# A Strassen FNet and MLP mix on one Trainium2 core: right-hand sums by adding DMAs, stored sums of x, and three more couples split twice

## The chip, the cores and the metric

The kernel runs on one core of a Trainium2 chip. Its time is the device time of one execution in microseconds (us), the median of several. The engines of the core that appear here are TensorE (PE, matmuls into PSUM), VectorE (DVE), ScalarE (ACT), GpSimd (POOL) and SyncE (SP). Here POOL and SP only issue DMAs, each from a queue of its own that runs in order; DVE, ACT and PE have in-order queues as well.

## The reference

```python
def reference(x, Cr, Ci, Wr, Wi, w1, b1, w2, b2, gate_w):     # x: 2048 x 1024, F = 3584
    g = sigmoid((x * gate_w).sum(-1, keepdims=True))
    a, b = x @ Wr.T, x @ Wi.T                                  # hidden transform, 1024 x 1024 each
    y = Cr @ a - Ci @ b                                        # sequence transform, 2048 x 2048 each
    h = relu(x @ w1 + b1) ** 2
    return g * y + (1 - g) * (h @ w2 + b2)                     # all float32
```

## The kernel before, in words

**Four products, five stages.** x W gives `ab` (x times both hidden matrices), C multiplies `ab` with the sequence matrices, K being real and imaginary part one behind the other (4096), the two h stages give h from w1 (2048 and 1536 features) and x, O multiplies w2 with h (K 3584). Intermediate results (`ab`, `gy`, `h`) go to HBM tiles and come back.

**Tiles.** A tile is 128 partitions x 2 x 512 float32, 512 KB, in one of 55 SBUF slots. It holds a K-step of 256 (2 x 128) by 512 rows or columns. Each operand tile is split into `hi` (rounded to fp32r, by ACT) and `lo` (what is left, by DVE; `Operand`, line 278 on), and each product is three matmuls: hi hi, hi lo, lo hi. Results gather in four pairs of PSUM banks (`Group`, line 337); ACT or DVE take them out.

**Strassen's form by Winograd.** Every stage cuts its matrices 2 x 2 and computes seven products instead of eight (`FACTORS`, line 40). The left factors need the sums S1 to S4 of left blocks, the right ones T1 to T4 of right blocks (`SUMS_L`, `SUMS_R`, lines 36 to 39); `Sums.of` (line 402) makes each once, as a `Part` (line 225): load two tiles (or one, if the other is a sum in SBUF), add or subtract on DVE. `T2` of C and O is written to an HBM tile `copy` by POOL and loaded again later (`FAR_TALL`). `seven` (line 425) runs the products in the order 1, 2, 5, 6, 3, 7, 4, and says how each is added to the four blocks of the result: a running value is put into PSUM ahead of the matmuls by ACT (`onto`), or added when the banks are taken out.

**Twice.** Some products are cut a second time by the same rule (`twice`). In `wide` (x W and h) these are products 1, 2, 5, 3 and 4, whole. In `tall` (C and O, where K is long) `TWICE_C` and `TWICE_O` say for how many couples of K-steps each product is cut again; the K-steps left over are done directly. Before, C has 1, 4, 4, 4 couples in products 1, 2, 3, 4 (of 8 K-steps), O 2, 3, 3, 3 (of 7). A couple cut again works with operands half as wide: names `both`, which hold hi and lo side by side.

**What sets the order.** The code records all operations first (`Queue`, line 123). `plan` (line 973) gives each a due time from its place ahead of the matmul that needs it, simulates the engines with the constants of lines 27 to 30, hands out the slots in that order, and writes down the order of each engine's queue; `emit` builds it. So any change of an operation or of a constant moves many others, and nothing is reordered at run time. Loads are issued by SP, stores by POOL. A store that nothing reads again (those of `out`) is due 20 us behind its place.

Of the kernel before, what the change touches and what calls it, by code (L numbers as in the profile page):

```python
# [44 lines left out]
def gated_mix_kernel(ctx: ExitStack, tc: tile.TileContext, x4, xn, w4, ct, w1a, w1b, w2, b1, b2, gw, out):  # L45
# [53 lines left out]
    class Op:  # L99


        def __init__(self, engine, name, args, kwargs):
            self.engine, self.name, self.args, self.kwargs = engine, name, args, kwargs
            sights = [a for a in (*args, *kwargs.values()) if isinstance(a, Sight)]
            outs = [a for a in (args[0], kwargs.get("accum_out")) if isinstance(a, Sight)]
            self.ins, self.outs = [a for a in sights if not any(a is o for o in outs)], outs
            n = max([a.size() for a in sights] + [0])
            self.load, self.end = 0.0, 0.0
            if name == "dma_start":
                self.time, self.load = ISSUE[engine], n * P * 4 / RATE[0]  # L110
            elif engine == "tensor":
# [113 lines left out]
    class Part(Near):  # L225


        def __init__(self, a, b=None, op=None, width=512):
            super().__init__("part")
            self.blocks, self.op, self.width, self.copy = ([a] if b is None else [a, b]), op, width, None  # L230
# [15 lines left out]
        def load(self, engines):  # L246
            run(self.load_parts(engines))

        def make_parts(self):
            for b in self.blocks:  # L250
                assert not isinstance(b, (Near, View)) or b.done
            src = [b.slot if isinstance(b, (Near, View)) else t for b, t in zip(self.blocks, self.slots)]
            mine = [t for t in self.slots if t is not None]
            self.slot, self.done = mine[0] if mine else take("sum"), True
            for k, c in self.cuts:
                if self.op:
# [138 lines left out]
    class Sums:  # L395


        def __init__(self, get, sums, keep=False, far=()):

            self.get, self.sums, self.keep, self.far, self.made = get, sums, keep, far, {}  # L400

        def of(self, key, width=512, near=False):
            if key in self.made:
                return self.made[key]
            if key not in self.sums:
# [4 lines left out]
            else:  # L410
                a, b, op = self.sums[key]
                e = Part(*(self.of(p, width).far() if p in self.far and not near else self.of(p, width) for p in (a, b)), op, width)
# [12 lines left out]
    def seven(order, second, new_u, c11, c12, c21, c22, put, add, direct, twice, slots, sign=1):  # L425

        one, u = new_u(), new_u()
        before = {p: order[:order.index(p)] for p in order}

        def product(p, old, new, ends, slots, drop=False, sign=1):  # L430
            if p in second:
                twice(p, old, new, ends, drop, sign)
                return

            direct(p, old, slots, lambda k, ps: put(new, k, ps, ends, sign), [new], sign, drop)
# [5 lines left out]
        def seven(k, ps):  # L441
            add(c22, k, ps, True, None, sign)
            if 4 in before[7]:
                add(c21, k, ps, True)
            else:
                put(u, k, ps)

        ends = {}
        for p in order:
# [6 lines left out]
            elif p == 4 and 7 in before[4]:  # L456
                product(4, u, c21, True, slots, True)
            elif p == 4:
                product(4, None, c21, False, slots)
            elif p == 5:  # L460
                product(5, None, c22, False, slots, sign=sign)
            elif p == 6:
                direct(6, one, 2 * slots, six, [u, c12], 1, 2 in before[6])
            else:
                direct(7, u, slots * (4 not in before[7]), seven, [u, c22, c21], 1, True)
# [5 lines left out]
    def tall(left, right, ksteps, order, second, first, target, final, last=None):  # L471
# [8 lines left out]
        right = {(q, c): Sums(lambda j, n, q=q, c=c: right_(j, n, q, c), SUMS_R, far=FAR_TALL) for right_ in (right,)  # L480
# [4 lines left out]
        def put(dst, k, ps, ends=False, sign=1):  # L485
            near = dst[k]
            near.slot or near.new()
            if ends:
# [4 lines left out]
            near.begun = True  # L493

        def add(dst, k, ps, ends=False, src=None, sign=1):
            near = dst[k]
            near.slot or near.new()
            nc.vector.tensor_tensor(flat(near.slot), flat((src or dst)[k].slot), flat(ps), op=ADD)
            near.begun = True
            if ends:  # L500
# [3 lines left out]
        def direct(p, onto, slots, take_up, into, sign, spend=False):  # L504
# [6 lines left out]
                            onto=onto and [onto[c, rp] for rp in range(2)], spend=spend, by_row=end and c) for c in range(2)]  # L511
            sts = {q: left[q].operand(l) for q in range(ksteps)}
            for q, c in sorted(((q, c) for q in range(ksteps) for c in range(2)), key=lambda e: e[::-1] if end else e):
                step(sts[q], right[q, c].operand(r), groups[c])
                if p == 6 and q < 2 * second.get(4, 0):
                    steps[-1][3].append(right[q, c].early("T4"))

        def twice(p, old, new, ends, drop, sign):
# [5 lines left out]
            if rest and (not old or p in first):  # L524
                some = [Group(4, len(rest), (lambda rp, ps, c=c: put(new, (c, rp), ps, sign=sign), 2 * (old is not new),
                                             [new[c, rp] for rp in range(2)]),
                              onto=old and [old[c, rp] for rp in range(2)], spend=drop) for c in range(2)]
# [4 lines left out]
                old, rest, drop = new, (), False  # L532
# [10 lines left out]
            l2 = {q: Sums(lambda m, j, q=q: View(base[j, q], 256 * m), SUMS_L, True) for q in range(k)}  # L543
            r2 = {q: Sums(lambda j, c, q=q: right[2 * q + j, c].of(r), SUMS_R, True) for q in range(k)}

            def one(_, ps):
                if old:
                    tmp[0, 0].new()
                    nc.scalar.activation(flat(tmp[0, 0].slot), flat(ps), AF.Copy)
                    add(new, block(0, 0), ps, src=old)  # L550
# [5 lines left out]
            def onward(dst, key, ps):  # L556

                if old:
# [3 lines left out]
                    nc.vector.tensor_tensor(flat(at), flat(old[key].slot), flat(u), op=ADD)  # L562
# [16 lines left out]
            def five(_, ps):  # L579
                key = block(1, 1)  # L580
                add(new, block(0, 1), ps)
                if old:
                    at = new[key].slot or new[key].new()
                    nc.vector.tensor_tensor(flat(at), flat(old[key].slot), flat(ps), op=ADD)
# [5 lines left out]
                    if ends and not more:  # L590
# [25 lines left out]
            for q in range(k):  # L616
                again = Sums(lambda j, c, q=q: right[2 * q + j, c].of(r), SUMS_R, True)
# [22 lines left out]
    def wide(left, right, rows, order, second, target, final, sign=1, onto_old=False):  # L640
# [9 lines left out]
        left = {(m, q): Sums(lambda i, j, m=m, q=q: left_(i, j, m, q), SUMS_L, far=FAR_WIDE) for left_ in (left,)  # L650
                for m in range(2) for q in range(2)}
        right = {(q, c): Sums(lambda j, n, q=q, c=c: right_(j, n, q, c), SUMS_R, far=FAR_WIDE) for right_ in (right,)
                 for q in range(2) for c in range(2)}
# [6 lines left out]
        def put(dst, k, ps, ends=False, sign=1):  # L660
# [3 lines left out]
            if ends:  # L664
# [4 lines left out]
            near.begun = True  # L669

        def add(dst, k, ps, ends=False, src=None, sign=1):
# [3 lines left out]
            nc.vector.tensor_tensor(view(near.slot, k), view((src or dst)[k].slot, k), view(ps, k),  # L675
                                    op=ADD if sign > 0 else SUB)
            near.begun = True
            if ends:
# [3 lines left out]
        def direct(p, onto, slots, take_up, into, sign, spend=False):  # L682
            l, r = FACTORS[p]
            mvs = [[right[q, c].operand(r) for q in range(2)] for c in range(2)]
            for m in range(2):
                sts = [left[m, q].operand(l, rows * P) for q in range(2)]
                for c in (m, 1 - m):
                    group = Group(rows, 2, (lambda rp, ps, m=m, c=c: take_up((m, c, rp), ps), slots,
                                             [d[m, c, rp] for d in into for rp in range(2)]),
                                  onto=onto and [onto[m, c, rp] for rp in range(2)], spend=spend, sign=sign)  # L690
# [3 lines left out]
        def twice(p, old, new, ends, drop, sign):  # L694

            l, r = FACTORS[p]
            l2 = Sums(lambda m, q: left[m, q].of(l, rows * P), SUMS_L, True)
            r2 = Sums(lambda q, c: right[q, c].of(r), SUMS_R, True)

            def takes(first, m, c, ends=False):  # L700
                def f(rp, ps):
# [3 lines left out]
                    elif old:  # L705
                        add(new, k, ps, ends, old, sign)
# [15 lines left out]
            begin = ((5, other), (1, chain))  # L722
            for p2, group in (*(begin if steps else begin[::-1]), (3, other), (6, chain), (2, last), (7, chain),
# [5 lines left out]
              sign)  # L729

    ab = {(n, q, c): Kept(f"ab{n}{q}{c}") for n in range(2) for q in range(8) for c in range(2)}

    def x_stage():
# [12 lines left out]
        wide(lambda i, j, m, q: x4[2 * i + m, j, q], lambda j, n, q, c: w4[n, c, j, q], 4, WIDE, TWICE_X, target, final, -1, True)  # L748
# [5 lines left out]
    def h_stage(part):  # L754
# [13 lines left out]
        def final(dst, ps, sign):  # L768
            kept, at, tiles, tile0 = to[dst]
            for k in range(tiles):  # L770
# [6 lines left out]
             WIDE, TWICE_H[part], target, final)  # L777
# [56 lines left out]
    def c_stage():  # L834
# [16 lines left out]
        tall(lambda i, j, q: ab[j, q, i], lambda j, n, q, c: ct[n, c, j, q], 8, TALL_C, TWICE_C, FIRST_C, target, final)  # L851
# [3 lines left out]
    def o_stage():  # L855
# [41 lines left out]
        ends = tall(lambda i, j, q: w2[i, j, q], lambda j, n, q, c: h_far[j, q, 2 * n + c], 7, TALL_O, TWICE_O, FIRST_O, target, final, last)  # L897
        return at, rows, fetched, ends
# [12 lines left out]
    at, rows, fetched, ends = o_stage()  # L911
# [61 lines left out]
def plan(ops, count, start):  # L973
# [196 lines left out]
```

## Time and profile before

| | us |
|---|---|
| three runs | 1867.46 median, 1867.27 to 1867.59 |
| the profiled execution | 1867.58 |
| its span, first to last instruction | 1865.3 |
| first wide matmul, from the span's start | 6.45 |
| x W, C, first h, second h, O, each to about | 289, 864, 1142, 1352, 1858 |

The granted clock of TensorE is 0.998 of full speed. The DMA queues moved 445.05 MB, SP's 365.10 and POOL's 78.14. Nearly all instructions carry the line in `emit` where they are built (L1128 before; the changed file is longer, and there it is L1194), so groups are told apart by operation and tile: `sum<-raw` is a sum of two loaded tiles into a third slot, `raw<-raw` one in place, `lo<-raw,hi` the split, `ps<-hi,lo` a matmul, `u`, `h`, `ab`, `y`, `o` results. In the rows, a count stands behind x, a mean time in ns behind the bar's first number, and the idle time of that engine just before, with what ended it, at the end.

### The profile page before, as it was taken

What the parts mean: (1) busy time and instruction counts of PE and PEld (TensorE: products, weight loads), DVE (VectorE), ACT (ScalarE), POOL (GpSimd) and SP (SyncE); (2) the same over time, 40 slices, a digit from 0 to 9 for tenths busy, and PEclk for the clock granted to TensorE, in tenths of its full rate; (3) what the DMA queues carried; (4) which work ended last, traced back from release to release, by engine and by line L of the source; (5) the groups of instructions that cost most, each with busy time, mean ns of one, the idle gap of its engine ahead of it and who ended that gap; (6) DMA issues with size and microseconds to landing.
All of it is one profiled execution on the core that took longest, in us unless ns stands there. A gap on an engine that the chain in (4) does not pass through costs nothing.

```text
span 1865.3 us, 22218 instructions
## 1 busy us (share of the span) xinstructions
PE 1850.1 (99%) x8162; PEld 1528.2 (82%) x8162; DVE 1760.2 (94%) x1728; ACT 1075.9 (58%) x1224; POOL 87.9 (5%) x162
## 2 busy tenths in 40 slices
PE   9999999999999999999999999999999999999998
PEld 7888888888888888888888888788888888888886
DVE  8997999799989899999997999999999999899988
ACT  6474654464343455466585798767976535364442
POOL 0000100000000000000000010000100001000000
PEclk9999999999999999999999999999999999999999
DMA  5741879349897379434552855737664799739943
GB/s 204 255 162 65 341 291 385 136 161 379 297 357 299 122 267 410 183 141 159 203 183 100 313 204 199 254 113 272 252 245 173 289 387 343 281 104 384 371 139 122
DMA packets 128861, 445.05 MB, mean 239 GB/s; under 512 B 14176, under 2 KB 23664, under 8 KB 128752
## 3 DMA queue, kind: packets, MB, share of 16 engines
q1 hardware_dynamic: 106848, 365.10, 53.4%
q0 software_dynamic: 21616, 78.14, 10.6%
q8 instruction: 64, 1.05, 0.2%
q10 hardware_dynamic: 288, 0.39, 0.1%
q14 instruction: 45, 0.37, 0.1%
HBM read 364.92 MB, written 78.65 MB: 238 GB/s over the span
## 4 chain that ended last, share of the span: by engine, by line
PE 84%; ACT 7%; DVE 6%; issue 2%; DMA 1%; SPq 0%; ACTq 0%; DVEq 0%
PE ps L1128 84%; ACT h L1128 3%; ACT hi L1128 3%; DVE lo L1128 2%; DVE h L1128 1%; DVE sum L1128 1%; ACT u L1128 1%; DVE raw L1128 1%; DMA raw<-in_x 1%; ACT ps L1128 0%; DVE o L1128 0%; DMA raw<-in_w 0%; DVE ab L1128 0%; DVE u L1128 0%; SPq L1128 0%
## 5 line engine op out<-in xcount | busy, mean ns | idle before, releaser
L1128 PE MATMUL ps<-hi 128*128 128x512 f32 x2034 | 792.2, 390 | 6.3 <-ACT hi L1128 3.1
L1128 PE MATMUL ps<-hi,lo 128*128 128x512 f32 x2034 | 791.2, 389 | 1.3 <-DVE lo L1128 1.3
L1128 PE MATMUL ps<-lo,hi 128*128 128x512 f32 x2034 | 790.9, 389 | 0.0
L1128 ACT ACTIVATE hi<-raw 128x1024 fp32r<-128x1024 f32 (+2 forms) x384 | 392.7, 1035 | 322.5 <-DVE raw L1128 183.9
L1128 DVE TENSOR_TENSOR lo<-raw,hi 128x1024 fp32r<-128x1024 f32 (+2 forms) x384 | 451.7, 1195 | 15.7 <-ACT hi L1128 10.7
L1128 PEld LDWEIGHTS ps<-hi 128*128 128x128 f32 x2034 | 382.2, 188 | 88.7 <-ACT hi L1128 3.7
L1128 PEld LDWEIGHTS ps<-hi,lo 128*128 128x128 f32 x2034 | 381.9, 188 | 81.7 <-DVE lo L1128 2.2
L1128 PEld LDWEIGHTS ps<-lo,hi 128*128 128x128 f32 x2034 | 382.0, 188 | 79.6 <-DVE lo L1128 0.4
L1128 PE MATMUL ps<-hi,both 128*128 128x512 f32 x1344 | 415.2, 389 | 0.1
L1128 DVE TENSOR_TENSOR raw<-raw 128x1024 f32<-128x1024 f32 (+1 forms) x276 | 324.3, 1203 | 8.6 <-DMA raw<-in_ct 6.3
L1128 ACT ACTIVATE hi<-sum 128x1024 fp32r<-128x1024 f32 x216 | 220.7, 1034 | 180.2 <-DVE sum L1128 121.7
L1128 PEld LDWEIGHTS ps<-hi,both 128*128 128x128 f32 x1344 | 252.2, 188 | 53.2 <-DVE both L1128 0.5
L1128 DVE TENSOR_TENSOR lo<-sum,hi 128x1024 fp32r<-128x1024 f32 (+1 forms) x216 | 254.8, 1195 | 14.5 <-PE ps L1128 12.0
L1128 PE MATMUL ps<-lo,both 128*128 128x512 f32 x672 | 261.4, 389 | 0.0
L1128 DVE TENSOR_TENSOR sum<-raw 128x1024 f32<-128x1024 f32 (+2 forms) x156 | 160.8, 1038 | 17.2 <-PE ps L1128 14.7
L1128 ACT ACTIVATE u<-ps 128x1024 f32<-128x1024 f32 (+1 forms) x116 | 112.4, 972 | 79.9 <-PE ps L1128 62.4
L1128 PEld LDWEIGHTS ps<-lo,both 128*128 128x128 f32 x672 | 126.1, 188 | 26.1
L1128 DVE TENSOR_TENSOR sum<-raw,sum 128x1024 f32<-128x1024 f32 (+2 forms) x117 | 128.4, 1099 | 1.9 <-PE ps L1128 0.6
L1128 DVE TENSOR_TENSOR h<-h,ps 128x1024 f32<-128x1024 f32 (+1 forms) x92 | 98.2, 1081 | 7.4 <-ACT u L1128 5.9
L1128 ACT ACTIVATE both<-sum 128x512 fp32r<-128x512 f32 x96 | 58.7, 623 | 69.9 <-DVE sum L1128 48.9
L1128 ACT ACTIVATE ps<-u 128x1024 f32<-128x1024 f32 (+1 forms) x80 | 78.0, 977 | 23.9 <-DVE u L1128 5.8
L1128 ACT ACTIVATE h<-h,b1c 128x512 f32<-128x512 f32 x112 | 76.1, 710 | 11.2 <-DVE h L1128 11.2
(49 smaller groups left out, 726.5 us busy)
## 6 DMA issues: line engine op xcount, KB each, us to landing
raw<-in_ct SPq DMA_DIRECT2D x153, 512.0 KB, 7.1
raw<-h SPq DMA_DIRECT2D x134, 512.0 KB, 7.1
raw<-in_x SPq DMA_DIRECT2D x107, 512.0 KB, 4.8
raw<-in_w SPq DMA_DIRECT2D x98, 512.0 KB, 6.8
raw<-ab SPq DMA_DIRECT2D x72, 512.0 KB, 7.5
h<-h POOLq DMA_DIRECT2D x48, 512.0 KB, 4.9
raw<-in_w1a SPq DMA_DIRECT2D x36, 512.0 KB, 5.1
ab<-ab POOLq DMA_DIRECT2D x32, 512.0 KB, 6.3
```

What stands on the lines that cost most here:

```text
L1128: made = getattr(real[op.engine], op.name)(*(actual(a) for a in op.args), **{k: actual(v) for k, v in op.kwargs.items()})
```

## The change

- `TWICE_C` and `TWICE_O` get an entry for product 5: two couples in C, one in O. In products cut for some couples only, the remaining K-steps now join the second cut's groups, except in product 2 (`first`).
- The signs of S and T are turned so that T1 and T3 are sums of two blocks as they lie in HBM (the old sums stay as `SUMS_L2`, `SUMS_R2` for the second cut). Products 4 and 6 come out negated, and the code that takes them up subtracts (`less`).
- A sum on the list `lands` is made in one slot: SP loads one tile into it, and when that has landed POOL issues a DMA that adds the second tile from HBM onto it (`accum_op=ADD`). `LAND_X`, `LAND_C`, `LAND_H`, `LAND_O` say for how many of a stage's K-steps and column halves T1 and T3 are made so: 6, 24, 4 and 4, 14, together 52.
- In h the roles of the two sides are exchanged (`flip`), so that x has the S sums in x W and in h. x W stores its sixteen (`shared`, `far`), and the h stages load them.
- The planner prices an adding DMA at 0.85 us of issue and 2.1 times the transfer (`ADDING`), and `out` stores are due 80 instead of 20 us behind their place (`LATE`).

```diff
-TWICE_X, TWICE_C, TWICE_O = (1, 2, 5, 3, 4), {1: 1, 2: 4, 3: 4, 4: 4}, {1: 2, 2: 3, 3: 3, 4: 3}
+TWICE_X, TWICE_C, TWICE_O = (1, 2, 5, 3, 4), {1: 1, 2: 4, 3: 4, 4: 4, 5: 2}, {1: 2, 2: 3, 3: 3, 4: 3, 5: 1}
+LAND_X, LAND_C, LAND_H, LAND_O = {"T1": 4, "T3": 2}, {"T1": 16, "T3": 8}, ({"T1": 4}, {"T1": 2, "T3": 2}), {"T1": 14}
+SHARE = ("S1", "S2", "S3", "S4")
+ADDING = 0.85, 2.1
+LATE = 80.0
-SUMS_L = {"S1": ((1, 0), (1, 1), ADD), "S2": ("S1", (0, 0), SUB), "S3": ((0, 0), (1, 0), SUB),
+SUMS_L = {"S1": ((1, 0), (1, 1), SUB), "S2": ((0, 0), "S1", SUB), "S3": ((1, 0), (0, 0), SUB),
           "S4": ((0, 1), "S2", SUB)}
-SUMS_R = {"T1": ((0, 1), (0, 0), SUB), "T2": ((1, 1), "T1", SUB), "T3": ((1, 1), (0, 1), SUB),
-          "T4": ((1, 0), "T2", SUB)}
+SUMS_R = {"T1": ((0, 1), (0, 0), ADD), "T2": ((1, 1), "T1", ADD), "T3": ((1, 1), (0, 1), ADD),
+          "T4": ((1, 0), "T2", ADD)}
...
         def load(self, engines):
-            run(self.load_parts(engines))
+            if self.lands:
+                self.slots = [take("raw")]
+                a, b = (b.at if isinstance(b, Kept) else b for b in self.blocks)
+                at = self.slots[0][:, :, 0:self.width]
+                next(engines).dma_start(at, a)
+                nc.gpsimd.dma_start(at, b, accum_op=ADD)
+            else:
+                run(self.load_parts(engines))
...
         def of(self, key, width=512, near=False):
             if key in self.made:
                 return self.made[key]
+            if self.shared and key in self.shared:
+                return self.shared[key]
...
+                if self.shared is not None and key in SHARE:
+                    self.shared[key] = e.far()
...
             elif p == 4 and 7 in before[4]:
-                product(4, u, c21, True, slots, True)
+                product(4, u, c21, True, slots, True, less=-1)
...
-                direct(6, one, 2 * slots, six, [u, c12], 1, 2 in before[6])
+                direct(6, one, 2 * slots, six, [u, c12], 1, 2 in before[6], -1)
...
-            if rest and (not old or p in first):
+            if rest and p in first:
...
+        if flip:
+            left = {(m, q): Sums(lambda j, i, m=m, q=q: left_(i, j, m, q), SUMS_R, far=FAR_WIDE, lands=spread(lands, 2 * q + m, 4))
+                    for left_ in (left,) for m in range(2) for q in range(2)}
+            right = {(q, c): Sums(lambda n, j, q=q, c=c: right_(j, n, q, c), SUMS_L, shared=shared[c, q])
+                     for right_ in (right,) for q in range(2) for c in range(2)}
...
-            op.due = op.near + 20.0
+            op.due = op.near + LATE
```

More of the change, by code (lines that the diff above doesn't have):

```diff
@@ L423, in early, with spread, seven, product @@
             return e
-    def seven(order, second, new_u, c11, c12, c21, c22, put, add, direct, twice, slots, sign=1):
+    def spread(lands, i, n):
+        return [key for key, k in lands.items() if (i + 1) * k // n > i * k // n]
+    def seven(order, second, new_u, c11, c12, c21, c22, put, add, direct, twice, slots, sign=1, flip=False):
+        c12, c21 = (c21, c12) if flip else (c12, c21)
         one, u = new_u(), new_u()
         before = {p: order[:order.index(p)] for p in order}
-        def product(p, old, new, ends, slots, drop=False, sign=1):
+        def product(p, old, new, ends, slots, drop=False, sign=1, less=1):
             if p in second:
-                twice(p, old, new, ends, drop, sign)
+                twice(p, old, new, ends, drop, sign, less)
                 return
-            direct(p, old, slots, lambda k, ps: put(new, k, ps, ends, sign), [new], sign, drop)
+            direct(p, old, slots, lambda k, ps: put(new, k, ps, ends, sign), [new], sign, drop, less)
         def six(k, ps):
@@ L442, in seven @@
             add(c22, k, ps, True, None, sign)
[L443 to L446, printed above, removed]
+            put(u, k, ps)
         ends = {}
@@ L514, in direct, with twice @@
                 step(sts[q], right[q, c].operand(r), groups[c])
-                if p == 6 and q < 2 * second.get(4, 0):
+                if p == 6 and q < 2 * second.get(4, 0) and "T4" not in right[q, c].lands:
                     steps[-1][3].append(right[q, c].early("T4"))
-        def twice(p, old, new, ends, drop, sign):
+        def twice(p, old, new, ends, drop, sign, less=1):
             l, r = FACTORS[p]
@@ L689, in direct, with twice @@
                                              [d[m, c, rp] for d in into for rp in range(2)]),
-                                  onto=onto and [onto[m, c, rp] for rp in range(2)], spend=spend, sign=sign)
+                                  onto=onto and [onto[m, c, rp] for rp in range(2)], spend=spend, sign=sign * less)
                     for q in range(2):
                         step(sts[q], mvs[c][q], group)
[L694 to L698, printed above, removed]
+        def twice(p, old, new, ends, drop, sign, less=1):
+            l, r = factors[p]
+            l2 = Sums(lambda m, q: left[m, q].of(l, rows * P), SUMS_L2, True)
+            r2 = Sums(lambda q, c: right[q, c].of(r), SUMS_R2, True)
             def takes(first, m, c, ends=False):
@@ L705, in f @@
                     elif old:
-                        add(new, k, ps, ends, old, sign)
+                        add(new, k, ps, ends, old, sign, less)
                         if drop:
```

130 lines of the change are left out of this document (86 added, 44 removed).

## The prediction

> **What bounds the kernel now.** I read the page first: busy time by engine and the chain that ended last; the rows below are its first line and the first line of its part 4.
>
> ```profile
> PE 1850.1 (99%) x8162; PEld 1528.2 (82%) x8162; DVE 1760.2 (94%) x1728; ACT 1075.9 (58%) x1224; POOL 87.9 (5%) x162
> ...
> PE 84%; ACT 7%; DVE 6%; issue 2%; DMA 1%; SPq 0%; ACTq 0%; DVEq 0%
> ```
>
> PE is busy throughout and holds most of the chain, DVE follows at 94%, POOL has almost nothing to do. Since a busy PE need not be at its peak, I went to the chain in order of time (start, length, what) for the long stretches in which PE waited for nobody:
>
> ```profile
> 100.12 941.02 PE ps L1128 x4150
> ...
> 1350.68 466.61 PE ps L1128 x2058
> ```
>
> 941.02 / 4150 = 0.2268 us and 466.61 / 2058 = 0.2267 us from one matmul to the next: **226.75 ns is the price of a matmul**. The page counts 8162 of them, 44 of which are the small warm-up ones of the start; 8118 x 0.22675 = 1840.8 us of the 1865.3 us span. What is left is 24.5 us, and the windows by stage say where it is (length, then busy time and count of PE, PEld, DVE, ACT, POOL, then clock, DMA share, GB/s). In order: x W, C (the sequence transform), the two h stages, O (h W2):
>
> ```profile
> 6.40:288.80 282.40, 278.82 (x1218) 229.47 (x1219) 266.67 (x244) 161.95 (x166) 16.21 (x30) 0.99 0.61 226
> 288.80:864.00 575.20, 575.20 (x2540) 476.27 (x2539) 536.29 (x542) 280.69 (x316) 16.59 (x31) 1.00 0.67 253
> 864.00:1142.00 278.00, 277.63 (x1224) 229.26 (x1223) 264.94 (x235) 203.97 (x231) 17.16 (x33) 1.00 0.55 199
> 1142.00:1352.00 210.00, 207.19 (x910) 170.02 (x909) 202.56 (x209) 167.08 (x216) 15.62 (x29) 1.00 0.62 221
> 1352.00:1858.00 506.00, 505.92 (x2232) 418.44 (x2231) 485.67 (x496) 259.99 (x295) 21.39 (x35) 1.00 0.69 259
> ```
>
> Length less count x 0.22675 gives the time lost to PE: 282.40 - 276.2 = 6.2 in x W, nothing in C, 278.00 - 277.5 = 0.5 and 210.00 - 206.3 = 3.7 in the two h stages, nothing in O. With 6.4 us ahead of the first matmul and 7.3 us behind the last window that is the 24.5, to the rounding. What PE waits for (whom, us in total, times, longest):
>
> ```profile
> PE ps L1128 <- ACT hi L1128: 3.1, 2, 2.2
> PE ps L1128 <- DVE h L1128: 2.6, 4, 0.9
> PE ps L1128 <- DVE lo L1128: 1.3, 2, 1.1
> PE ps L1128 <- DVE ones L1128: 1.1, 1, 1.1
> PE ps L1128 <- DVE u L1128: 0.5, 1, 0.5
> ```
>
> hi and ones belong to the start, where data must first arrive; lo is mainly one gap at 98.62 us in x W. The h and u rows, 3.1 us in five waits, are the h stages: there PE waits for a PSUM bank that DVE has not emptied. With restarts they are the 4.2 us (0.5 + 3.7) of the windows. DVE in the second h stage is busy 202.56 of 210.00 us. So PE bounds everywhere, and DVE touches it in the h stages alone.
>
> **Part 1: three couples of K split twice.** A couple is two K-tiles by two column halves: 2 x 2 x 24 = 96 matmuls; split once more it is seven products of 12, that is 84. Two couples more in C and one in O: 36 matmuls fewer. The built programs agree: 8118 before, 8082 after (C 2532 to 2508, O 2220 to 2208). C and O are the stages where nothing is lost to PE, so each of the 36 is worth its full price: 36 x 0.22675 = **-8.2 us**. These durations price what DVE does for it:
>
> ```profile
> 94.39 2.27 DVE sum L1128 x2
> ...
> L1128 DVE TENSOR_TENSOR raw<-raw 128x1024 f32<-128x1024 f32 x260 | 309.7, 1219 | 8.6 <-DMA raw<-in_ct 6.3 <-DMA raw<-ab 1.3 <-DMA raw<-h 0.6
> L1128 DVE TENSOR_TENSOR both<-sum,both 128x512 fp32r<-128x512 f32 x96 | 64.5, 685 | 4.4 <-ACT both L1128 4.4
> ```
>
> One wide tensor_tensor takes 1219 ns, but two in a row took 2.27 us, so 1.14 each in a queue that is full; a narrow one 0.69. A couple split once needs 12 wide ones (2 left sums, 4 right sums, 6 lo): 13.7 us of DVE beside 96 x 0.22675 = 21.8 us of PE. Split twice, with its T1 sums landing by DMA, it needs about 13 wide and 11 narrow ones: 22.4 us beside 19.0. That alone would put DVE 3.4 us behind per couple; but the T1 sums of the other K-tiles of product 5 land too, so such a couple falls to 8 wide ones, 9.1 us beside 21.8. Product 5 of C then asks DVE for 2 x 22.4 + 2 x 9.1 = 63 us beside 82 of PE. So I cost the extra work at nothing; without the landing each couple takes 4.6 us more, 81 us beside 82, and DVE has no slack left in that product.
>
> **Part 2: sums by adding DMAs, and stored sums of x.** Counted in the two programs: 52 sums of two HBM tiles leave DVE (6 in x W, 24 in C, 4 and 4 in h, 14 in O); 32 sums of x leave it in the h stages, 16 in each, where a stored sum is loaded instead (48 loads of x go, 32 of the copies come, x W stores 16). DVE has 1714 instructions before and 1678 after: by width 65 wide fewer, 4 of 768 columns fewer, 33 narrow more. 65 x 1.14 + 4 x 0.95 - 33 x 0.69 = 55 us of DVE less, of 1760. By the order, 14 instructions go in each h stage, where it matters: at 1.14 us that is 16 of 202.56 us in the second one, which leaves DVE at 187 beside 206.3 us of matmuls, 91% instead of 98%. What this can give back is the h stages' 4.2 us and no more. ACT stays as loaded there as before (167.08 of 210.00), and the last wait, as h ends, is behind ACT's relu and square too; I take three quarters: **-3.2 us**. Bounds: 0 if ACT is as late as DVE was, -4.2 if all goes; -1.4 more if the gap at 98.62 goes as well.
>
> Each adding DMA stands on POOL's queue, waits there for the plain load on SP's queue to land, and must land before ACT or DVE reads the tile. The trace has no adding DMA. The nearest rows are plain ones of the same size (KB, us from issue to landing) and POOL's issue (count, busy, mean ns):
>
> ```profile
> raw<-in_ct SPq DMA_DIRECT2D x153, 512.0 KB, 7.1
> ...
> copy<-raw POOLq DMA_DIRECT2D x30, 512.0 KB, 6.9
> raw<-copy SPq DMA_DIRECT2D x30, 512.0 KB, 4.4
> ...
> L1128 POOL DMA_DIRECT2D copy<-raw x30 | 16.1, 536 | 166.3 <-DVE raw L1128 166.3
> ```
>
> Lower end: a plain one, 7 us. Upper end: read and write one after the other, twice that, 14 us. I take 10, nearer the plain row, as most of 7 us is not transfer: 512 KB at 200 to 260 GB/s is 2 to 2.6 us. To be late, an adding DMA must miss its place. In the built program's order (all engines in one list) the matmuls between the adding DMA and the first reader of its tile, times 0.22675, are 6.1 us at the least, 11 for the tenth, 15 in the middle; to the first matmul that needs the result 21 at the least and 37 in the middle. At 10 us four readers of 52 are a little late, on engines that have 21 us or more until PE notices: 0. At 14 us seventeen are late by up to 8 us, still under 21: 0 to +2 us.
>
> Queued behind a waiting add on POOL are stores of ab, copies and h; they hold slots, and the loads wait for slots. POOL gets 68 more issues (52 adds, 16 copies) x 0.54 = 37 us on top of 87.9. SP loses 68, so the number of large transfers is the same; if each adding one moves its bytes twice, 52 x 0.52 MB = 27 MB come to
>
> ```profile
> DMA packets 128861, 445.05 MB, mean 239 GB/s; under 512 B 14176, under 2 KB 23664, under 8 KB 128752
> ```
>
> 6% more, on DMA engines that are 55 to 69% used by stage. Costed at 0.
>
> The Trainium skill, Collectives: The Full Stack, section "The bandwidth ceiling", says that an add in the DMA path costs no cycles of its own but a second read on the same ring, which makes a reduce about half as fast as a copy (1.93 measured there). As an estimate by that page an adding DMA is 2 to 2.6 us of transfer longer than a plain one, which changes nothing in the sum; no run here shows it yet.
>
> A page speaks against the move to POOL: the Trainium skill, SBUF — State Buffer, section "SBUF: two separate sides", says that a DMA issued by GpSimd starves while DVE runs an operation in a 2-port mode, and "Who interferes with whom" there excepts tensor_tensor, nearly all of DVE's work here. The trace agrees with the exception: copy<-raw issues in 536 ns with DVE 94% busy, and lands in 6.9 us beside 7.1 for SP's loads. Were it otherwise, the time would go as in rival B below.
>
> **Part 3: signs, and due times.** The sign changes swap ADD for SUB or the order of operands; no count changes but 6 u sums (wide) that go, counted above: 0. Stores that nobody reads get a later due time. In the order, 14 DVE operations on o (6 wide, 8 like the row below) now stand from the 95th to the 41st matmul before the end, where they came earlier before.
>
> ```profile
> L1128 DVE SCALAR_TENSOR_TENSOR o<-o,b2c,g 128x512 f32<-128x512 f32 x10 | 7.1, 746 | 0.1
> ```
>
> 6 x 1.14 + 8 x 0.75 = 13 us of DVE within 55 x 0.22675 = 12.5 us: DVE is full there for a moment, with one lo among them. The last 36 matmuls and what follows them stand in the same order as before, so the tail stays as it is: 0, +2 at most.
>
> **Sum**, against the profiled execution: span 1865.3 - 8.2 - 3.2 = 1853.9. That execution took 1867.58 with 2.3 us around its span, and the median of three runs is 1867.46, 0.1 below it: 1853.9 + 2.3 - 0.1 = 1856.1; I say **1856.0**.
>
> **Rivals.**
> A, only the matmuls pay: DVE has slack in h, but PE's waits there hang on ACT, which is 86.08 us busy in 92 at the end of the first h stage:
>
> ```profile
> 1050.00:1142.00 92.00, 91.63 (x403) 75.23 (x402) 89.93 (x82) 86.08 (x105) 9.68 (x19) 1.00 0.66 243
> ```
>
> Then 1867.46 - 8.2 = 1859.3. For it: that row; against it: the four waits name DVE's h. Small new waits of up to 4 us belong here, so 1858 to 1863.5.
> B, the adding DMAs are too slow in a row, and it ends slower. The order has 20 of them within 86 us in C (410 to 496 by matmuls) and 14 within 73 us in O, one per 4.3 and 5.2 us. With the 37 us ahead of PE it decides from (86 + 37) / 20 = 6.2 us per add on. At 8 us each (one add's whole latency exposed, no two in flight) C is late by 20 x 8 - 86 - 37 = 37 us and O by 14 x 8 - 73 - 37 = 2: 1867.5 - 8.2 + 39 = 1898. For it: adds are unmeasured and queued behind stores. Against: plain POOL stores overlap, and 512 KB at the rates above is 2.6 us.
> C, product 5's denser DVE work is not hidden, because PE meets it with nothing prepared ahead: each of the three couples costs the 3.4 us by which DVE is behind, 10 us in all, and the gain is eaten: 1867.5 - 8.2 + 10 = 1869. Against it: nothing is lost to PE in C and O before.
>
> **Chances.** Forecast 0.70, with its own range 1852 to 1858.5; A 0.15; C 0.04; B 0.11. A measurement tells about 0.2%, 3.7 us, from no change: faster means below 1863.7. Faster 0.70 + 0.15 = 0.85, same 0.04, slower 0.11. The range reaches from all waits gone (1867.46 - 8.2 - 4.2 - 1.4 = 1853.7, less 2 for the start) to the end of A: 1851.5 to 1864.
>
> **What would show it.** Right: 8126 PE instructions at 226.75 ns; windows of the h stages without loss, DVE near 90% there; PE's waits on DVE h gone; C and O still without loss; tile raw<-in_ct on POOL landing under about 12 us. Wrong: PE waiting for hi or lo in C or O near the rows of adds, ACT hi waiting for DMA raw by tens of us, POOL waiting with loads behind it.

## The result and the profile after

The changed kernel takes 1858.56 us (median of six runs, 1856.91 to 1859.77) against 1867.39 (six runs) before: 8.8 us less, ratio 0.9952, 95% interval 0.9940 to 0.9965. It is faster, inside the forecast range and 2.6 us above the forecast time. The profiled execution is the slowest of the six, 1859.77 with a span of 1858.0.

The first line of the page, and its first chain line, changed kernel:

```profile
PE 1841.6 (99%) x8126; PEld 1521.0 (82%) x8126; DVE 1706.1 (92%) x1692; ACT 1096.3 (59%) x1254; POOL 143.3 (8%) x230
...
PE 86%; ACT 5%; DVE 4%; issue 3%; DMA 1%; POOL 0%; SPq 0%; DVEq 0%; POOLq 0%; ACTq 0%
```

PE lost the 36 instructions, DVE 54 us, POOL gained 55. What PE waits for, same columns as before:

```profile
PE ps L1194 <- ACT hi L1194: 4.7, 3, 2.3
PE ps L1194 <- ACT u L1194: 1.1, 1, 1.1
PE ps L1194 <- DVE ones L1194: 1.1, 1, 1.1
PE ps L1194 <- DVE lo L1194: 1.0, 2, 0.6
PE ps L1194 <- DVE h L1194: 0.8, 1, 0.8
PE ps L1194 <- DVE u L1194: 0.6, 1, 0.6
```

The h and u rows have not gone: 2.5 us where there were 3.1, and one of them now names ACT. The third hi wait, 1.0 us, belongs to them: it stands in the second h stage too, at the last step of its last product, so that PE waits 3.5 us in the h stages. The windows of the stages:

```profile
288.80:860.00 571.20, 570.15 (x2515) 471.56 (x2514) 526.98 (x543) 288.21 (x330) 36.08 (x52) 1.00 0.72 251
860.00:1138.00 278.00, 277.87 (x1225) 229.45 (x1224) 251.13 (x223) 210.88 (x239) 22.23 (x39) 1.00 0.57 193
1138.00:1348.00 210.00, 206.36 (x904) 168.97 (x903) 185.49 (x195) 164.36 (x213) 20.25 (x33) 1.00 0.58 192
1348.00:1852.00 504.00, 503.22 (x2219) 416.16 (x2217) 477.64 (x490) 265.68 (x303) 33.52 (x50) 1.00 0.73 262
```

In the second h stage DVE is down to 185.49 us of 210, as forecast (187), and PE still loses 210.00 - 904 x 0.22675 = 5.0 us there. C loses a little now: 571.20 - 2515 x 0.22675 = 0.9.

Windows cut by time are a little blunt. The table below counts sharply, for every kernel of this study: time from the first matmul of a stage to the first of the next, less the stage's matmuls x 0.22675. x W includes the 3.5 to 5 us of the start.

| kernel | wide matmuls | x W | C | first h | second h | O | us, median |
|---|---|---|---|---|---|---|---|
| before | 8118 | 6.3 | -0.2 | 0.9 | 4.1 | 0.4 | 1867.4 |
| changed | 8082 | 4.5 | 1.4 | 0.6 | 5.4 | 0.1 | 1858.56 |
| e1, couples alone | 8082 | 6.3 | 15.8 | 0.8 | 4.2 | 6.9 | 1881.73 |
| e2, all but the couples | 8118 | 3.6 | 1.4 | 0.6 | 4.3 | -0.2 | 1865.65 |
| e3, changed, other step order | 8082 | 5.0 | 2.1 | -0.1 | 1.6 | 1.0 | 1857.05 |
| e4, before, other step order | 8118 | 4.6 | -0.2 | -0.1 | 0.7 | 0.5 | 1861.31 |
| e5, no adding DMAs | 8082 | 6.3 | 9.4 | 0.6 | 3.6 | 4.5 | 1871.68 |
| e6, no stored sums | 8082 | 4.8 | 1.4 | 1.3 | 5.8 | 4.0 | 1864.52 |
| e7, all T1 and T3 landed | 8082 | 3.6 | 10.6 | 2.2 | 4.3 | 7.1 | 1884.06 |
| e8, due times as before | 8082 | 3.5 | 1.4 | 0.6 | 5.2 | 4.8 | 1862.47 |
| e9, e3 with spread gates | 8082 | 3.5 | -0.2 | -0.1 | 1.6 | 1.1 | 1853.71 |
| e10, e9, third couple in C | 8070 | 4.4 | 9.5 | -0.1 | 1.6 | 1.0 | 1861.10 |
| e11, e10, second couple in O | 8058 | 5.0 | 9.7 | -0.1 | 0.8 | 4.1 | 1861.37 |
| e12, e9 without stored sums | 8082 | 4.4 | -0.2 | -0.1 | 0.7 | 4.5 | 1857.42 |

Each single trace carries some luck of a few tenths to 1.5 us, above all at the start. The kernel before had medians of 1867.1 to 1867.4 in the experiments.

### The profile page after: what moved, and what is told of

Same layout as the page of the kernel before. It is cut to its first block, busy times and chain, and to the rows that moved or that the text cites. A ratio compares the mean times of both kernels' runs of the same rounds, so it can differ in the third digit from the quotient of the medians.

```text
span 1858.0 us, 22135 instructions
## 1 busy us (share of the span) xinstructions
PE 1841.6 (99%) x8126; PEld 1521.0 (82%) x8126; DVE 1706.1 (92%) x1692; ACT 1096.3 (59%) x1254; POOL 143.3 (8%) x230
## 3 DMA queue, kind: packets, MB, share of 16 engines
q0 software_dynamic: 31920, 113.27, 19.5%
q8 instruction: 64, 1.05, 0.2%
## 4 chain that ended last, share of the span: by engine, by line
PE 86%; ACT 5%; DVE 4%; issue 3%; DMA 1%; POOL 0%; SPq 0%; DVEq 0%; POOLq 0%; ACTq 0%
PE ps L1194 86%; ACT h L1194 2%; ACT hi L1194 2%; DVE lo L1194 1%; DVE h L1194 1%; DVE sum L1194 1%; DMA raw<-in_ct 0%; DMA h<-h 0%; DMA raw<-in_x 0%; ACT u L1194 0%; ACT ps L1194 0%; POOL h L1194 0%; DVE o L1194 0%; DVE u L1194 0%; DVE raw L1194 0%
## 5 line engine op out<-in xcount | busy, mean ns | idle before, releaser
L1194 PE MATMUL ps<-hi 128*128 128x512 f32 x1938 | 755.1, 390 | 7.5 <-ACT hi L1194 4.7
L1194 PE MATMUL ps<-hi,lo 128*128 128x512 f32 x1938 | 753.7, 389 | 0.6 <-DVE lo L1194 0.6
L1194 PE MATMUL ps<-lo,hi 128*128 128x512 f32 x1938 | 753.9, 389 | 0.4 <-DVE lo L1194 0.4
L1194 PE MATMUL ps<-hi,both 128*128 128x512 f32 x1512 | 467.0, 389 | 0.0
L1194 PEld LDWEIGHTS ps<-hi 128*128 128x128 f32 x1938 | 364.2, 188 | 86.7 <-ACT hi L1194 4.3
L1194 PEld LDWEIGHTS ps<-hi,both 128*128 128x128 f32 x1512 | 283.8, 188 | 59.3 <-ACT ps L1194 0.4
L1194 PE MATMUL ps<-lo,both 128*128 128x512 f32 x756 | 294.1, 389 | 0.0
L1194 DVE TENSOR_TENSOR lo<-sum,hi 128x1024 fp32r<-128x1024 f32 (+1 forms) x228 | 269.0, 1196 | 18.5 <-PE ps L1194 10.2
L1194 DVE TENSOR_TENSOR raw<-raw 128x1024 f32<-128x1024 f32 (+1 forms) x192 | 227.8, 1203 | 13.1 <-DMA raw<-h 3.6
L1194 ACT ACTIVATE u<-ps 128x1024 f32<-128x1024 f32 x110 | 106.4, 971 | 101.3 <-PE ps L1194 81.1
L1194 ACT ACTIVATE ps<-u 128x1024 f32<-128x1024 f32 x82 | 80.1, 978 | 24.7 <-DVE u L1194 6.9
```

Source lines behind the costliest of these rows:

```text
L1194: made = getattr(real[op.engine], op.name)(*(actual(a) for a in op.args), **{k: actual(v) for k, v in op.kwargs.items()})
```

## The experiments

The theory after the result: the 36 matmuls paid in full, because the landed sums gave DVE the room for them; the h stages gave nothing back, because PE waits there for one bank of PSUM between two steps and not for a busy DVE. The rival: it is DVE's load, and 91% is still too much.

**e1 and e2, the change taken apart.** e1 is the kernel before with the three couples alone, e2 the changed kernel without them.

```diff
 e1, in the kernel before
-TWICE_X, TWICE_C, TWICE_O = (1, 2, 5, 3, 4), {1: 1, 2: 4, 3: 4, 4: 4}, {1: 2, 2: 3, 3: 3, 4: 3}
+TWICE_X, TWICE_C, TWICE_O = (1, 2, 5, 3, 4), {1: 1, 2: 4, 3: 4, 4: 4, 5: 2}, {1: 2, 2: 3, 3: 3, 4: 3, 5: 1}
 e2, in the changed kernel: the same edit taken back
```

> The kernel before with part 1 alone: product 5 split twice for two couples in C and one in O, all sums on DVE as before. If the 36 matmuls pay in full and what was prepared ahead hides DVE's extra work: 1867.4 - 8.2 = 1859.2 us, nothing lost to PE in C and O. If the extra DVE work (27 us per couple beside 19.0 us of matmuls) needs the landed sums to hide it: 1861 to 1870, with PE waiting for lo or hi in product 5 of C and O.

> The changed kernel without part 1, so 8118 wide matmuls again: adding DMAs, stored sums, signs and due times alone. By the prediction's step for the h stages (DVE's load makes PE wait there): 1867.4 - 3.2 = 1864.2. If PE's waits in the h stages hang on a PSUM bank being emptied between two steps on the same banks, whatever DVE's load: 1866 to 1868, the h stages lose 4 to 6 us as before.

e1 took 1881.73 us (1880.51 to 1882.16), ratio 1.0076 (1.0064 to 1.0089): 14 us slower with 36 matmuls fewer. What PE waits for in e1:

```profile
PE ps L1128 <- DVE lo L1128: 9.7, 12, 1.9
PE ps L1128 <- ACT hi L1128: 3.1, 2, 2.2
PE ps L1128 <- DVE h L1128: 2.6, 4, 0.9
```

Twelve waits for lo, where there were two; the table has 15.8 us lost in C and 6.9 in O. Counted in the same way by product, only 3.4 of the 15.8 are lost in product 5 and 1.2 in product 6, and 11.3 in product 3, which comes behind them and which the edit leaves as it was; in O 6.6 of the 6.9 stand in product 3. So the loss comes mostly behind product 5, the one product that I had priced. e2 took 1865.65 (1864.87 to 1866.94), ratio 0.9992 (0.9984 to 1.0001): the adding DMAs, stored sums and due times alone are not to be told from nothing. So neither half is worth anything by itself, and together they are worth 8.8 us.

**e5, no adding DMAs.** All else of the change stays.

```diff
-LAND_X, LAND_C, LAND_H, LAND_O = {"T1": 4, "T3": 2}, {"T1": 16, "T3": 8}, ({"T1": 4}, {"T1": 2, "T3": 2}), {"T1": 14}
+LAND_X, LAND_C, LAND_H, LAND_O = {}, {}, ({}, {}), {}
```

> The changed kernel with no adding DMA: all 52 sums loaded as two tiles and added on DVE, stored sums of x and the three couples kept. If the three couples pay only because the landed sums free DVE in C and O: 1865 to 1880 us, PE waiting for lo in C and O as when the couples were added alone (1881.7). If the couples alone lost for another reason, such as the order of their steps in the kernel before: 1858 to 1860.

1871.68 us (1870.68 to 1871.99), ratio 1.0024 (1.0014 to 1.0033), 13.1 us above the changed kernel: 9.4 lost in C, 4.5 in O. Its C window beside that of the changed kernel above:

```profile
288.80:860.00 571.20, 565.95 (x2479) 464.28 (x2479) 552.08 (x568) 292.55 (x331) 15.48 (x29) 1.00 0.66 253
```

DVE is at 552 of 571 us there, 97%, against 527. PE stalled at 97% and not at 92%; of the 9.4 us, 6.5 are lost in product 5 and 3.1 in product 1. The share by itself is not the reason: in e4 below DVE is at 97% of a stage and PE loses next to nothing.

**e7, every T1 and T3 by an adding DMA**, 84 instead of 52.

```diff
-LAND_X, LAND_C, LAND_H, LAND_O = {"T1": 4, "T3": 2}, {"T1": 16, "T3": 8}, ({"T1": 4}, {"T1": 2, "T3": 2}), {"T1": 14}
+LAND_X, LAND_C, LAND_H, LAND_O = ({"T1": 4, "T3": 4}, {"T1": 16, "T3": 16}, ({"T1": 4, "T3": 4},) * 2,
+                                  {"T1": 14, "T3": 14})
```

> The changed kernel with every T1 and T3 made by an adding DMA, 84 instead of 52 (X 8, C 32, h 8 and 8, O 28). If adding DMAs cost nothing as long as the DMA engines keep up, and DVE no longer bounds: 1858.6 within 2. If they are too slow in a row (the prediction's rival B, from 6.2 us per add on): 1865 to 1900, with ACT or DVE waiting for raw from POOL's queue.

1884.06 us (1883.17 to 1885.05), ratio 1.0091 (1.0077 to 1.0104). DVE has less to do than in the changed kernel (1672.8 us busy instead of 1706.1), and the kernel is 25 us slower than that one: 10.6 lost in C, 7.1 in O, and 12.0 us instead of 3.5 from the last matmul's start to the last instruction. The worst place in C, 690 to 740 us, in the changed kernel and then in e7:

```profile
690.00:740.00 50.00, 50.00 (x222) 41.43 (x221) 41.57 (x37) 20.58 (x20) 6.54 (x9) 1.00 1.04 365
```

```profile
690.00:740.00 50.00, 43.58 (x192) 35.80 (x192) 27.67 (x25) 15.49 (x16) 9.10 (x12) 0.97 1.05 322
```

The DMA engines are full in both (share 1.04 and 1.05), but with 8 adds instead of 5 they move 322 GB/s instead of 365. DMA issues in that window (KB, us to landing), the changed kernel first:

```profile
raw<-in_ct SPq DMA_DIRECT2D x12, 512.0 KB, 15.8
raw<-ab SPq DMA_DIRECT2D x10, 512.0 KB, 14.8
raw<-in_ct POOLq DMA_DIRECT2D x5, 512.0 KB, 8.4
```

```profile
raw<-in_ct SPq DMA_DIRECT2D x8, 512.0 KB, 22.7
raw<-in_ct POOLq DMA_DIRECT2D x8, 512.0 KB, 14.2
raw<-ab SPq DMA_DIRECT2D x8, 512.0 KB, 22.7
```

The plain loads are the victims: 22.7 us to landing where it was 15, and DVE waits for ab (21.5 us in four waits between 690 and 745 us). This is what the prediction's rival B feared, in the DMA engines rather than in POOL's queue, and it sets in between 52 and 84 adds. The loss in O and at the end was not followed up.

**e3 and e4, the order of the steps in h.** In a product cut twice, steps 7 and 4 used the same banks one behind the other. The other order has none such. e3 is the changed kernel, e4 the kernel before with this edit.

```diff
             chain = Group(rows, 1, takes(True, 0, 0), takes(False, 0, 1, ends), takes(False, 1, 1, ends),
                           takes(True, 1, 0, ends))
-            other = Group(rows, 1, takes(True, 1, 1), takes(True, 0, 1))
...
+            chain = Group(rows, 1, takes(True, 0, 0), takes(True, 0, 1), takes(False, 1, 1, ends),
+                          takes(True, 1, 0, ends))
+            other = Group(rows, 1, takes(True, 1, 1), takes(False, 0, 1, ends))
...
-            for p2, group in (*(begin if steps else begin[::-1]), (3, other), (6, chain), (2, last), (7, chain),
-                              (4, chain)):
+            for p2, group in ((1, chain), (5, other), (6, chain), (3, other), (7, chain), (2, last), (4, chain)):
```

> The changed kernel with the seven steps of a product cut twice in x W and h in the order 1, 5, 6, 3, 7, 2, 4, so that no two steps in a row use the same PSUM banks (before: 7 and 4 did). If PE's waits in the h stages are the emptying of a bank between steps 7 and 4: the gaps at the last step of each product cut twice go, 1858.6 - 5 = 1853.5, with DVE as busy as before in the h stages. If they come from DVE's or ACT's load: no change, 1858.6, with gaps elsewhere.

> The kernel before with the same order of steps, 1, 5, 6, 3, 7, 2, 4, and DVE as loaded as ever (98% in the second h stage). Emptying of a bank: the h stages' 4.2 us go, 1867.4 - 4 = 1863.4. DVE's load: no change, 1867.4.

Why this border: five gaps of the second h stage stand before its matmuls 108, 234, 360, 630 and 900, in the kernel before (3.6 us in all) and in the changed one (3.4 us) alike. The changed one has a sixth, 1.25 us before matmul 810, where PE waits for ACT to take u out of a bank. A step is 18 matmuls there, a product cut twice 126, product 6 and 7 144 each: 126 - 18 = 108, 126 + 108 = 234, 252 + 108 = 360, and so on, always the last step of a product cut twice. The kernel before at the second of them, PE alone, then DVE in the same moment:

```profile
1194.83 0.39 PE L1128 MATMUL ps<-hi,lo 128*128 128x512 f32 x1
...
1196.19 0.39 PE L1128 MATMUL ps<-hi,lo 128*128 128x512 f32 x1
1197.45 0.47 PE L1128 MATMUL ps<-hi 128*128 128x512 f32 x1 [0.87 <-DVE h L1128]
```

```profile
1194.96 1.22 DVE L1128 TENSOR_TENSOR raw<-raw 128x1024 f32<-128x1024 f32 x1
1196.09 1.81 DVE L1128 TENSOR_TENSOR h<-h,ps 128x1024 f32<-128x1024 f32 x2
```

With three blocks of rows, six matmuls (1.36 us) lie between the last one into the first pair of banks and the next step's first one into it, and DVE needs 1.2 us for the add that empties it, after it is told. With four blocks (first h) there are twelve, and the gaps were small. How long a gap gets depends on what DVE is doing: here the last matmul into the pair starts at 1194.83, DVE is in another operation and comes to the add 1.26 us later, and PE loses 1.0 us; before matmul 630 it comes 0.43 us behind, and PE loses 0.2. So the order opens the gap, and DVE's queue sets its length.

e4 took 1861.31 us (1860.35 to 1861.83), ratio 0.9966 (0.9952 to 0.9979), 6.1 us off. By the table 4.4 of them are the h stages', and 1.7 are x W's, whose steps the edit orders anew as well. Its second h stage:

```profile
1140.00:1348.50 208.50, 208.10 (x918) 172.00 (x917) 203.22 (x211) 167.61 (x217) 16.16 (x30) 1.00 0.64 226
```

DVE is busy 203.22 of 208.50 us, 97%, and PE loses 208.50 - 918 x 0.22675 = 0.3. So the load alone does not make PE wait. e3 took 1857.05 (1856.16 to 1858.0), ratio 0.9945 (0.9932 to 0.9957), 1.5 below the changed kernel: less than the 5 expected, though all six gaps are gone. The runs of the two overlap, so that this gain is not clear of the noise. One new one of 1.5 us stands in the first product, where PE waits for ACT to fill a bank, and C lost 2.1 in its trace and O 1.0; the median of the changed kernel also lies 1.2 below its profiled run.

**e9, the gates spread.** What C loses in the changed kernel it loses before two matmuls at 308.4 and 309.5 us. DVE there, changed kernel:

```profile
304.79 1.22 DVE L1194 SCALAR_TENSOR_TENSOR raw<-raw,gwb 128x1024 f32<-128x1024 f32 x1
305.94 0.08 DVE L1194 DVE_READ_ACCUMULATOR raw<-raw,gwb 128x1 f32 x1
305.94 1.22 DVE L1194 SCALAR_TENSOR_TENSOR raw<-raw,gwb 128x1024 f32<-128x1024 f32 x1
307.08 0.08 DVE L1194 DVE_READ_ACCUMULATOR raw<-raw,gwb 128x1 f32 x1
307.08 2.35 DVE L1194 TENSOR_TENSOR lo<-raw,hi 128x1024 fp32r<-128x1024 f32 x2
```

PE waits for these two lo (the lo row above, two waits, 1.0 us). DVE takes them up the moment the gate sums ahead of them end, and nobody needs those sums yet.

```diff
-        want(at + 2 + t // 2, Gate(t))
-    want(at + 24, *rows)
+        want(at + 14 + 3 * t // 2, Gate(t))
+    want(at + 42, *rows)
```

> The kernel with the steps in the order 1, 5, 6, 3, 7, 2, 4 (1857.05 us), and the sixteen gate operations of DVE (1.14 us each) spread over the steps 14 to 37 of C instead of 2 to 10. If the gap of 2.3 us at 305 to 310 us is a lo that stands behind gate operations in DVE's queue: 1857.05 - 2 = 1855. If it is the late landing of ab or the matrix tiles: no change, the gap stays.

1853.71 us (1853.53 to 1854.95), ratio 0.9930 (0.9917 to 0.9944): 3.3 off e3, C's loss gone (2.3 us by the table; the rest is in the start of these two traces). It is the fastest kernel of the study, 13.6 us below the one before and 4.9 below the changed one.

**e6 and e12, no stored sums**, in the changed kernel and in e9.

```diff
-SHARE = ("S1", "S2", "S3", "S4")
+SHARE = ()
```

> The changed kernel without stored sums: the h stages make the 32 sums of x on DVE again (about 16 us more DVE in each). If DVE's load in h costs PE time, as the prediction's step has it: 1858.6 + 3.2 = 1861.8. If only the emptying of a bank does: 1858.6 within 1.5 either way, DVE above 95% in the second h stage, gaps at the same matmuls.

> The kernel with changed step order and spread gates (1853.71 us), without stored sums, so that the h stages make the 32 sums of x on DVE again. If, with the bank gaps gone, DVE's load in the h stages costs PE nothing: 1853.7 within 1. If the six us that the stored sums were worth in the changed kernel are DVE work that the end of h leaves to the start of O: 1856 to 1860, lost at the end of h and in the first 40 us of O.

e6: 1864.52 us (1862.17 to 1865.87), 6.0 above the changed kernel; e12: 1857.42 (1856.97 to 1857.56), 3.7 above e9. My theory said that e6 would lose nothing, and it lost 6 us. The table says where they go: the h stages lose 0.7 and 0.4 us more in e6, where the gaps of the old order are still there to be lengthened, nothing more in e12, where they are not, and O loses 4.0 and 4.5 where it lost 0.1 and 1.1. e12, the second h stage and the 40 us behind it:

```profile
1136.00:1345.00 209.00, 208.60 (x921) 172.48 (x920) 204.46 (x213) 167.88 (x219) 21.84 (x36) 1.00 0.66 225
1345.00:1385.00 40.00, 37.40 (x158) 28.83 (x157) 39.36 (x44) 35.88 (x45) 2.16 (x4) 1.00 0.88 301
```

DVE at 98% costs PE nothing inside h. But at the start of O, where product 1 begins with its two couples, DVE and ACT are full, and what was not prepared ahead in h is missing. The last part is a reading: in e9 they are about as full in these 40 us (39.76 and 37.34), and O loses 1.1.

**e8, the due times as before.**

```diff
-LATE = 80.0
+LATE = 20.0
```

> The changed kernel with stores that nobody reads due 20 instead of 80 us behind their place, as before. If the due times are worth nothing, as the prediction costs them: 1858.6 within 1. If they keep DVE free for PE at the end of O: 1860 to 1862, with O losing time to PE near its end.

1862.47 us (1860.92 to 1863.78), 3.9 above the changed kernel. O loses 4.8, 3.9 of them in product 5 and most of these between 1500 and 1520 us, in the burst of adds for that product. The changed kernel has PE busy all of these 20 us; in e8 the window reads

```profile
1500.00:1520.00 20.00, 18.25 (x73) 14.34 (x72) 18.82 (x19) 8.27 (x9) 5.83 (x7) 0.91 1.04 332
```

POOL has seven DMAs there instead of four; `out` stores, due early, stand among the adds (between 1480 and 1530 us POOL waits 7.6 us for o of DVE, with adds behind it). That it is the queueing, and not the order of DVE alone, was not tried separately.

**e10 and e11, more couples in e9.**

```diff
 e10
-... 5: 2}, {1: 2, 2: 3, 3: 3, 4: 3, 5: 1}
+... 5: 3}, {1: 2, 2: 3, 3: 3, 4: 3, 5: 1}
 e11
+... 5: 3}, {1: 2, 2: 3, 3: 3, 4: 3, 5: 2}
```

> The kernel with changed step order and spread gates (1853.71 us), with a third couple of product 5 in C split twice: 12 matmuls fewer. If the landed sums still leave DVE room in C (529 of 571 us busy, a couple adds about 13): 1853.7 - 2.7 = 1851.0. If DVE is at its limit in product 5: 1853 to 1858, with PE waiting for lo or both in C.

> The same with a second couple in O besides: 24 matmuls fewer. If DVE has room in both stages: 1853.7 - 5.4 = 1848.3. If not in O, where it was busy 474 of 504 us: 1851 to 1856, with the loss in O.

1861.10 (1860.4 to 1861.7) and 1861.37 us (1860.24 to 1862.51): 7.4 and 7.7 slower than e9 with 12 and 24 matmuls fewer. In e10 the loss is in product 5 of C:

```profile
460.00:480.00 20.00, 14.30 (x61) 11.14 (x59) 19.93 (x24) 11.29 (x15) 3.14 (x4) 0.96 0.87 208
480.00:500.00 20.00, 18.61 (x74) 15.27 (x75) 18.55 (x20) 12.80 (x16) 1.72 (x2) 0.87 0.67 184
```

DVE is full and the DMA engines are not: one couple more tips C from no loss to 9.5 us. In e9 DVE is nearly as full from 460 to 480 us (19.69 of 20) and PE loses nothing; in e10 the chain that PE waits for is DVE work from 450 to 481 us, and the main gap is one wait of 5.6 us. In O the second couple's 12 matmuls (2.7 us) are eaten by 3.1 us of loss, which here stands in product 3 again.

## Why the prediction was right, point by point

- **36 matmuls, -8.2 us: right.** C and O stayed close to lossless, 1.4 and 0.1 us. The 1858.56 is 8.8 below the before, and the rest sums to about nothing: the traces lose 12.0 instead of 11.5 us.
- **The couples' extra DVE work at nothing, because the sums land: right, and more depends on it than I said.** I put the cover's worth at two figures that nearly met (81 us of DVE beside 82 of PE without it). Without it the kernel is 13 us slower (e5), and the couples alone 14 (e1): DVE at 97% of the stage is already too much in C. The adding DMAs are 13 of the 23 us between e1 and the changed kernel; taken away singly, the stored sums (e6) are worth 6 and the due times (e8) 4. That DVE's work comes in bursts in C is my reading of e10, whose DVE is full (19.93 of 20 us) just where PE stalls; it was not tried by itself. e1 shows that pricing one product was too narrow, as most of its loss comes in a later one.
- **The h stages, -3.2 us: wrong.** The step that failed is the one from "there PE waits for a PSUM bank that DVE has not emptied", which was so, to "What this can give back", which took the wait for a matter of DVE's load. DVE came down as forecast and the loss stayed (4.1 to 5.4 in the second h). It was the order of two steps on one pair of banks: e4 removes it with DVE at 97%. The trace before had the means to tell: the waits stand at the same step of each product, the first three of them 126 matmuls apart. The relief was worth something elsewhere, 3.5 to 3.9 us at the start of O (e6, e12), which the change needs and the kernel before did not lose. Why the old start of O got by without is open; product 1 began with its uncut K-steps there.
- **Adding DMAs, 10 us to landing: about right.** Measured, changed kernel:

```profile
raw<-in_ct POOLq DMA_DIRECT2D x24, 512.0 KB, 9.4
...
raw<-h POOLq DMA_DIRECT2D x14, 512.0 KB, 10.0
raw<-in_w POOLq DMA_DIRECT2D x6, 512.0 KB, 7.1
```

The eight adds of the h stages landed in 5.7 and 6.5 us. The adds issue in 0.87 us, not 0.54, so that POOL gained 55 us and not 37:

```profile
L1194 POOL DMA_DIRECT2D raw<-in_ct x24 | 20.8, 868 | 287.6 <-PE ps L1194 120.6 <-DVE sum L1194 87.0 <-DMA raw<-in_ct 43.9
```

As to their bytes, POOL's queue before moved 78.14 MB in 10.6% of 16 engines' span, and moves 113.27 MB in 19.5% now:

```profile
q0 software_dynamic: 31920, 113.27, 19.5%
```

Before that is 0.106 x 1865.3 / 78.14 = 2.53 us per MB; now, with 8.4 MB more of plain copies at that price, 362 - 219 = 143 us are left for the 26.7 MB of adds, 5.4 us per MB, **2.1 times a plain transfer**. e5, with the copies and without the adds, bears out the price of the plain ones: 86.53 MB in 11.8% of 1870.0 us are 2.55 us per MB. The Trainium skill, Collectives: The Full Stack, section "The bandwidth ceiling", puts the lower rate of a reduce down to a second read, with 1.93 as the ratio measured there; the trace agrees with the size, and no run here shows the cause.
- **Rival B: not here, but real.** With 84 adds (e7) the adds and loads are too slow in a row, with the DMA engines full and several adds in flight. Its figure of 6.2 us per add was not put to the test.
- **Rival C: not here, but real.** One couple more (e10), or the couples without the landed sums (e5), and product 5's DVE work is no longer hidden.
- **Due times at nothing: wrong in size.** e8 prices them at 3.9 us, in the bursts of adds in O and not in the tail I looked at. So the change needs them too.
- **The gap at 98.62 us: only among the bounds.** It is gone, and x W loses 4.5 us instead of 6.3. In e5, without adding DMAs, 1.3 us are lost again before the same matmul, the 386th of x W; with them nothing is lost there in any run (nor in e4, by the order of the steps alone). So landed sums of x W paid there, which the sum of the prediction leaves out; that this about makes up for the next point is luck.
- **C's start: not foreseen.** 1.4 us are lost there, in the changed kernel and in e2 alike; in the kernel before none. Product 1 now begins with its couple, and the gate sums stand in front of it.

So the forecast of 1856.0 was 2.6 too low by the h term, and the time is that of rival A, 1859.3, which had 0.15: 1858.56 lies at the upper edge of the forecast's own 1852 to 1858.5, and the stated range had room because it reached to the end of A. A's reason, waits on ACT, shows in the gap at matmul 810; the other five are the order's, and with the other order (e3) all six go.

## What to carry to other kernels

When an engine is bound by matmuls, cutting matmuls moves the work to the engine that prepares operands; price the two together, because each half alone may lose (here +14 us and -2, together -8.8). A wait that came back at the same step of a pattern was a matter of that step's order here, beside an engine that was 97% busy: see at which matmul the gaps stand before blaming the load. An adding DMA takes work from VectorE at about twice the DMA time of a plain transfer (2.1 times here), so spend it where the DMA engines have room, and stop before they are full.

## What the runs showed of the hardware that I had not expected

After a gap, PE's next matmuls can be slow for some microseconds, so that a stall costs more than its length. e1, PE alone:

```profile
676.66 0.50 PE L1128 MATMUL ps<-lo,both 128*128 128x512 f32 x1 [1.89 <-DVE lo L1128]
677.26 0.97 PE L1128 MATMUL ps<-hi,both 128*128 128x512 f32 x2
678.03 0.63 PE L1128 MATMUL ps<-lo,both 128*128 128x512 f32 x1
678.46 1.05 PE L1128 MATMUL ps<-hi,both 128*128 128x512 f32 x2
679.31 0.63 PE L1128 MATMUL ps<-lo,both 128*128 128x512 f32 x1
```

From 677.6 to 680.6 us the starts lie 0.427 us apart instead of 0.227, after a wait of 1.89 us with shorter ones ahead of it. In e6 one wait of 1.99 us at 1164.35 us was followed by eight such steps, with no other gap in the 29 us ahead of it. The granted clock falls to 0.91 in e8's window above and to 0.87 in e10's. A gap of 1.3 us by itself, as in the kernel before at 1196 us, is followed by the normal pace after one matmul. The Trainium skill, TensorE: Matmul & The Clock Gate, section "Part 1: The HAM clock gate", has the half clock (426.7 ns for this width) behind an idle window of some 3.4 us; the spacing agrees, and here gaps of 2 us and less were enough.
